# Windowed attention into a Fourier-mixing MLP: folding both DFTs by symmetry, reloading q and k as row runs

## The chip, the cores and the metric

The kernel runs on one core of a Trainium2 chip. Its engines are TensorE (PE, with its weight loads PEld), VectorE (DVE), ScalarE (ACT), GpSimd (POOL) and SyncE (SP); 16 DMA engines move data. The metric is device microseconds for one launch: 533.88 us, the median of three runs (532.82 to 534.48).

## The reference, cut to what matters

Inputs are q, k, v of shape (4 batches, 8 heads, 768 rows, 64), eight memory keys and values for each head, and the MLP's weights 512x2048 and 2048x512. Outputs are (4, 768, 512), all float32.

```
for c in range(24):                                  # chunks of 32 query rows
    k_full = concat(mem_k, k[32c-16 : 32c+40])       # clipped at the ends; v_full alike
    a = softmax(q[32c : 32c+32] @ k_full.T / 8)
    out[32c : 32c+32] = a @ v_full
x = heads side by side                               # (4, 768, 512)
mixed = real(fft(fft(x, axis=1), axis=2))
u  = x + mixed
un = (u - mean(u)) / sqrt(var(u) + 1e-6)             # over the 512 columns
y  = u + relu(un @ w_ch1) @ w_ch2
```

The real part of the two-dimensional DFT is C768 x C512 - S768 x S512, with C and S the cosine and sine tables. So it is two matrix products with 768-row tables, then two with 512-row tables.

## The kernel before, in words

Engines run their own instruction streams in order. The code is written per batch, and a scheduler fixes each stream's order at compile time: it interleaves the attention of batch b+1 with the Fourier part of batch b, as far as buffers allow. The calls at the end are attention(0), then for each b attention(b+1) and fx(b).

**Attention** (`emit_attention`, L148 to L215). Heads go in pairs. POOL issues DMAs that load q, k and v and cast on the way (L157 to L181); in DRAM one row of a head is 256 bytes. PE transposes q and k in 128-row tiles (L168, L172), ACT copies them to `qkTx`. Scores `p12` come in twelve blocks of 96 keys by 64 queries for each head (L194), and the memory keys are two more matmuls with 32 columns of weights (L187, L190). ACT takes two exponentials (L198, L200), PE multiplies by v with a column of ones (L205, tile `xa`, one PSUM buffer), and DVE divides by the sum (L212, L213), a reciprocal and a product for each 64-row half. The result lies in `xsb`, of which there are three, one for each batch in flight.

**Fourier part** (`emit_fx`, L217 to L284). x is split into fp16 high and low parts (`xh` L227, `xl` L228). For each of four 128-column tiles, 12 matmuls for the cosine (`pa`) and 12 for the sine (`pb`), each 392 columns wide (L236, L238), give the row DFT transposed for rows 0 to 391; the other rows follow by reflection. ACT and DVE split these into high and low again (L241 to L244), and DVE writes reflected copies `rrev` (L249). The column DFT (L267) is 16 matmuls of 512 columns for each of six row tiles `kt`, into `pm`. DVE then adds x (L270), takes mean and variance (L272, L273), ACT and DVE take 1/sqrt (L275, L276) and DVE subtracts the mean (L277). After all six tiles, PE transposes (L283) and DVE copies (L284) to `unT`.

**MLP** (L286 to L303). Two halves of 384 rows: 16 groups of four matmuls with relu on ACT (L290, L293), then three groups of 16 matmuls of 512 columns (L298). The factor 1/sqrt(var) is applied on DVE at the output (L301), where u is added too.

All matmul accumulators of fx share the tag `acc` in `fps`, with two PSUM buffers. The tables come from Sin on ACT at the start (L114, L118), beside the first attention; each switch between Sin and Exp loads a table. The two weight DMAs are the first on POOL's queue (L125, L126).

Of the kernel before, what the change touches and what calls it, by code (L numbers as in the profile page):

```python
# [10 lines left out]
FP32 = mybir.dt.float32  # L12
BF16 = mybir.dt.bfloat16
# [8 lines left out]
BIGM = 800.0  # L22


@with_exitstack
def kernel(
# [52 lines left out]
    tmem = cpool.tile([P, 2], FP32)
    nc.gpsimd.affine_select(out=tmem, in_=mbias, compare_op=ALU.is_ge, fill=0.0,  # L80
                            base=95, pattern=[[0, 2]], channel_multiplier=-1)
    nc.gpsimd.affine_select(out=mbias, in_=tmem, compare_op=ALU.is_ge, fill=-BIGM / 8.0,
                            base=103, pattern=[[0, 2]], channel_multiplier=-1)

    xsb = {}

    cs_sb = wpool.tile([P, NST, KM], FP16)
    ss_sb = wpool.tile([P, NST, KM], FP16)
    cd_sb = wpool.tile([P, NDT, DM], FP16)
    nsd_sb = wpool.tile([P, NDT, DM], FP16)  # L90
    sd_sb = wpool.tile([P, NDT, DM], FP16)
    krep = cpool.tile([P, S], FP32)
    nc.gpsimd.iota(krep, pattern=[[1, S]], base=0, channel_multiplier=0,
                   allow_small_or_imprecise_dtypes=True)
    with tc.tile_pool(name="trig", bufs=1) as tpool:
        def gen_trig(n_free, nt, NN, cout, sout, neg_sin):
            inv = 1.0 / float(NN)
            sc = 2.0 * math.pi / NN
            for t in range(nt):
                sv = tpool.tile([P, 1], FP32, tag="sv")  # L100
                nc.gpsimd.iota(sv, pattern=[[1, 1]], base=t * P, channel_multiplier=1,
                               allow_small_or_imprecise_dtypes=True)
                tsb = tpool.tile([P, 512], FP32, tag="tsb", bufs=1)
                ysb = tpool.tile([P, 512], FP32, tag="ysb", bufs=1)
                rsb = tpool.tile([P, 512], FP32, tag="rsb", bufs=1)
                tt = tsb[:, 0:n_free]
                yt = ysb[:, 0:n_free]
                rt = rsb[:, 0:n_free]
                nc.vector.tensor_scalar(tt, krep[:, 0:n_free], sv, None, ALU.mult)
                nc.vector.tensor_scalar(yt, tt, inv, None, ALU.mult)  # L110
                nc.vector.tensor_scalar(rt, yt, FSC, FSC, ALU.add, ALU.subtract)
                nc.vector.scalar_tensor_tensor(rt, rt, float(NN), tt, ALU.mult, ALU.subtract)
                ssc = sc if neg_sin else -sc
                nc.scalar.activation(sout[:, t, 0:n_free], rt, AFT.Sin, bias=0.0, scale=ssc)  # L114
                nc.vector.tensor_scalar(yt, tt, inv, 0.25, ALU.mult, ALU.add)
                nc.vector.tensor_scalar(rt, yt, FSC, FSC, ALU.add, ALU.subtract)
                nc.vector.scalar_tensor_tensor(rt, rt, float(NN), tt, ALU.mult, ALU.subtract)
                nc.scalar.activation(cout[:, t, 0:n_free], rt, AFT.Sin, bias=hpi_b, scale=-sc)  # L118
        gen_trig(KM, NST, S, cs_sb, ss_sb, neg_sin=False)
        gen_trig(DM, NDT, DM, cd_sb, nsd_sb, neg_sin=True)  # L120
    nc.vector.tensor_scalar(sd_sb, nsd_sb, -1.0, None, ALU.mult)
# [3 lines left out]
    nc.gpsimd.dma_start(w1_sb, moe_w_ch1.rearrange("(dt p) f -> p dt f", p=P))  # L125
    nc.gpsimd.dma_start(w2_sb, moe_w_ch2.rearrange("(ht p) m -> p ht m", p=P))  # L126

    qkTx = [apool.tile([P, KWQ + S], BF16, name=f"qkTx{i}") for i in range(NBUF)]
    va = [apool.tile([P, NT, 66], FP32, name=f"va_{i}") for i in range(2)]
    for i in range(NBUF):  # L130
        nc.vector.memset(qkTx[i][:, 0:LEFT], 0.0)
        nc.vector.memset(qkTx[i][:, LEFT + S:KW + NMEM], 0.0)
        nc.vector.memset(qkTx[i][:, KW + NMEM:KWQ], 0.0)
    for i in range(2):
        nc.vector.memset(va[i][:, :, 0:66], 0.0)
        nc.vector.memset(va[i][0:96, :, 64:65], 1.0)
        nc.vector.memset(va[i][0:16, 0, 64:65], 0.0)
        nc.vector.memset(va[i][64:96, NT - 1, 64:65], 0.0)
        nc.vector.memset(va[i][64:80, NT - 1, 64:65], 1.0)
        nc.vector.memset(va[i][96:104, :, 64:65], 1.0)  # L140
# [76 lines left out]
    def emit_fx(b):  # L217
# [122 lines left out]
```

## Time and profile before

The page is of one profiled execution with a span of 530.8 us from the first instruction to the last. The page gives no separate total for it; the timed median is 533.88 us, so 3.1 us lie around the span.

| what | value |
|---|---|
| span of the profiled execution | 530.8 us |
| timed median (three runs) | 533.88 us |
| PE busy | 440.5 us, 83% |
| DVE, ACT, POOL busy | 207.6, 190.9, 146.8 us |
| chain that ended last, PE's share | 71% |
| of that L290, L298, L267 | 17%, 16%, 15% |

Busy times of PE count a matmul from its start to its modelled end, and matmuls overlap; the pace of a run of matmuls is read from the time of the run over its count. The chain's rows give this pace directly.

### The profile page before, as it was taken

To read this page: it belongs to the slowest core of one execution; us is meant where nothing else is said; L and a number is where in the kernel's file an instruction comes from. 1 tells how busy PE (TensorE), PEld (TensorE's weight loads), DVE (VectorE), ACT (ScalarE), POOL (GpSimd) and SP (SyncE) were. 2 spreads that over 40 slices of the span, in tenths; PEclk is the share of its full clock that TensorE was granted. 3 is DMA by queue.
4 is the path that set the end of the run, shared out by engine and by line. 5 is a ranking of instruction groups with operands and counts; after the bars stand their busy time and mean duration, and the time that the engine had idled before them with its cause. 6 is when DMAs were issued, how large, how long until landed. Compare 5 with 4: busy or idle time off the path is not lost.

```text
span 530.8 us, 7916 instructions
## 1 busy us (share of the span) xinstructions
PE 440.5 (83%) x3184; PEld 242.5 (46%) x3184; DVE 207.6 (39%) x451; ACT 190.9 (36%) x343; POOL 146.8 (28%) x218
## 2 busy tenths in 40 slices
PE   0044358688998999999989999989979997997996
PEld 0023236455554545556446455654444544444453
DVE  7246552533656022252861115347631042452101
ACT  2169884223343615243215251542032501004250
POOL 5356643576555100266522011520000000000000
PEclk9999999999999899999997999999979999999999
DMA  7968551395546211366513111710000110000101
GB/s 140 195 74 84 63 55 49 57 97 71 71 68 42 23 44 33 91 95 79 54 13 26 41 37 65 97 49 0 1 0 22 40 61 0 1 0 1 40 21 59
DMA packets 66243, 27.28 MB, mean 51 GB/s; under 512 B 57504, under 2 KB 60576, under 8 KB 66208
## 3 DMA queue, kind: packets, MB, share of 16 engines
q0 software_dynamic: 58400, 19.58, 29.7%
q1 hardware_dynamic: 7808, 7.21, 4.1%
q8 instruction: 25, 0.41, 0.3%
q14 instruction: 10, 0.08, 0.1%
HBM read 31.00 MB, written 6.29 MB: 70 GB/s over the span
## 4 chain that ended last, share of the span: by engine, by line
PE 71%; ACT 10%; DMA 5%; POOL 5%; issue 4%; DVE 4%; ACTq 0%; POOLq 0%
PE ph L290 17%; PE pc L298 16%; PE pm L267 15%; PE pa L236 5%; PE pb L238 4%; DMA w_sb<-in_moe_w_ch_dram 4%; PE xa L205 4%; PE p L194 4%; PE tp L283 2%; PE trp L172 2%; PE trp L168 1%; ACT L118 1%; ACT L198 1%; ACT L200 1%; PE p L187 1%
## 5 line engine op out<-in xcount | busy, mean ns | idle before, releaser
L290 PE MATMUL ph<-unT,w_sb 128*128 128x384 f16 x512 | 97.8, 332 | 1.5 <-ACT hT L293 0.7
L293 ACT ACTIVATE hT<-ph 128x384 f16<-128x384 f32 x128 | 62.4, 491 | 86.5 <-PE ph L290 86.5
L298 PE MATMUL pc<-w_sb,hT 128*128 128x512 f16 x384 | 84.2, 379 | 0.0
L290 PEld LDWEIGHTS <-w_sb 128*128 128x128 f16 x512 | 49.4, 98 | 42.0 <-issue 14.0
L301 DVE SCALAR_TENSOR_TENSOR osb<-pc,rstd_s,xsb 128x512 f32<-128x512 f32 x24 | 18.0, 750 | 117.4 <-PE pc L298 117.1
L298 PEld LDWEIGHTS <-hT 128*128 128x128 f16 x384 | 37.5, 98 | 44.9 <-issue 0.6
L205 PE MATMUL xa<-va,e 128*64 128x66 f32 x768 | 37.3, 255 | 23.7 <-ACT e L200 23.1
L205 PEld LDWEIGHTS xa<-va,e 128*64 128x64 f32 x768 | 31.7, 163 | 35.0 <-ACT e L200 24.3
L175 POOL DMA_DIRECT2D va<-in_v_dram x32 | 17.8, 555 | 107.1 <-PE xa L205 103.5
L176 POOL DMA_DIRECT2D va<-in_v_dram x32 | 25.8, 806 | 55.0 <-PE trp L163 40.8
L236 PE MATMUL pa<-cs_sb,xh 128*128 128x392 f16 x96 | 32.4, 337 | 10.4 <-DVE r1l L243 6.8
L212 DVE RECIPROCAL zsum<-xa 64x6 f32<-64x6 f32 x64 | 12.3, 192 | 61.5 <-PE xa L205 60.7
L213 DVE TENSOR_TENSOR xsb<-xa,zsum 64x384 f32<-64x384 f32 x64 | 35.5, 554 | 1.9
L236 PE MATMUL pa<-cs_sb,xl 128*128 128x392 f16 x96 | 32.2, 336 | 0.9 <-DVE xl L228 0.9
L238 PE MATMUL pb<-ss_sb,xl 128*128 128x392 f16 x96 | 32.3, 337 | 0.0
L238 PE MATMUL pb<-ss_sb,xh 128*128 128x392 f16 x96 | 32.3, 336 | 0.0
L194 PEld LDWEIGHTS <-qkTx 64*96 64x96 bf16 x384 | 24.6, 146 | 15.1 <-issue 10.2
L157 POOL DMA_DIRECT2D q2b<-in_q_dram x32 | 29.8, 931 | 6.1 <-PE trp L168 5.8
L275 ACT ACTIVATE rsq<-mu_s,eps_b 128x1 f32<-128x1 f32 x24 | 7.1, 295 | 66.8 <-DVE mu_s L273 66.8
L241 ACT CAST r<-pa 128x392 f16<-128x392 f32 x16 | 7.8, 486 | 63.4 <-PE pa L236 63.4
L159 POOL DMA_DIRECT2D k2b<-in_k_dram x32 | 29.0, 907 | 1.2 <-PE trp L172 1.1
L194 PE MATMUL p<-qkTx 64*96 64x64 bf16 x384 | 28.4, 229 | 0.7
(93 smaller groups left out, 612.7 us busy)
## 6 DMA issues: line engine op xcount, KB each, us to landing
out_dram<-osb SPq DMA_DIRECT2D x24, 256.0 KB, 2.0
va<-in_v_dram POOLq DMA_DIRECT2D x32, 176.0 KB, 3.4
w_sb<-in_moe_w_ch_dram POOLq DMA_DIRECT2D x2, 2048.0 KB, 17.4
q2b<-in_q_dram POOLq DMA_DIRECT2D x32, 96.0 KB, 3.2
k2b<-in_k_dram POOLq DMA_DIRECT2D x32, 96.0 KB, 3.3
va<-in_v_dram POOLq DMA_DIRECT2D x32, 88.0 KB, 2.9
va<-in_mem_v_dram SPq DMA_DIRECT2D x32, 24.0 KB
va<-in_v_dram SPq DMA_DIRECT2D x32, 4.0 KB, 1.8
```

The lines of the kernel that those rows point to most:

```text
L157: nc.gpsimd.dma_start(q2b[:, :, hj, :], q[b, h + hj].rearrange("(t p) d -> p t d", p=P))
L159: nc.gpsimd.dma_start(k2b[:, :, hj, :], k[b, h + hj].rearrange("(t p) d -> p t d", p=P))
L176: nc.gpsimd.dma_start(v1[0:64, 1:NT, 0:D], v[b, h, 48:48 + (NT - 1) * 64].rearrange("(t p) d -> p t d", p=64))
L194: nc.tensor.matmul(p12[0:96, t, :], kqx[r0:r1_, t * 64:t * 64 + 96], kqx[r0:r1_, KWQ + t * 64: KWQ + t * 64 + 64], start=True, stop=True, ...
L205: nc.tensor.matmul(xa[rr:rr + 64, t // 2, 0:66], e1[:, t, :], v1[:, t, :], start=True, stop=True)
L213: nc.vector.tensor_tensor(xsb[b][rr:rr + 64, :, hc:hc + D], xa[rr:rr + 64, :, 0:D], zs.unsqueeze(2).to_broadcast([64, NST, D]), ALU.mult)
L236: nc.tensor.matmul(pa[:, 0:KM], lx, cs_sb[:, st, :], start=(im == 0), stop=(im == nmm - 1))
L238: nc.tensor.matmul(pb[:, 0:KM], lx, ss_sb[:, st, :], start=(im == 0), stop=(im == nmm - 1))
L267: nc.tensor.matmul(pm, lhs, rhs[:, dt, :], start=(im2 == 0), stop=(im2 == nmm2 - 1))
L290: nc.tensor.matmul(ph[:, 0:384], w1_sb[:, dt, ts(ht, P)], unT[:, dt, sh * 384:(sh + 1) * 384], start=(dt == 0), stop=(dt == NDT - 1))
L293: nc.scalar.activation(hT[:, ht, :], ph[:, 0:384], AFT.Relu)
L298: nc.tensor.matmul(pc, hT[:, ht, ts(stl, P)], w2_sb[:, ht, :], start=(ht == 0), stop=(ht == NHT - 1))
```

## The change

It rewrites the tile function. What the new code does:

- **Loads.** q and k of a head pair come uncast, as fp32, in runs of eight rows (2 KB) to 96 partitions (`qf`, `kf`, two buffers); POOL casts them to bf16 (L231, L233). All q, k, v and memory loads are issued by SP (L108 to L119). The 32 rows of v that the next block shares are copied on POOL (L237) and not loaded twice. `va` has four buffers.
- **Weights.** Eight DMAs on POOL's queue after the third head pair (`emit_weights`).
- **Attention.** Eight transposes each for q and k; memory keys are transposed once for all heads (`emit_mem_keys`) and stand inside each 128-column key block, so the scores are twelve matmuls per head with 128 columns of weights (L259) and nothing else. One reciprocal and one product per head (L274, L276). `xsb` has two buffers.
- **Row and column DFT.** x is folded on DVE before the products. `zy` adds or subtracts the two column halves (even and odd output columns), `pq` adds or subtracts the two row halves (even and odd output rows), `ff` adds or subtracts the reflected columns. For each of two column parities the row DFT is 24 matmuls of 193 columns (L312), plus 12 with one column of weights at parity 0 (L319). The column DFT is 8 matmuls of 256 columns per row tile (L341).
- **Norm.** Each row tile is transposed as soon as its mean is taken off (L353). 1/sqrt(var) is taken on POOL once per batch (L356, L357).
- **Order.** The calls are now pairs of batch 0, fx(0), then for each b: pairs of b+1, fx(b+1), mlp(b). `acc` has three buffers and serves the transposes too. The tables are half as wide and use one row of Sin calls.

The core of the diff:

```diff
+        nc.sync.dma_start(qf[n % NS], q[b, h:h + 2].rearrange("h (p j) d -> p h (j d)", j=RB))
+        nc.sync.dma_start(kf[n % NS][2:2 + QP], k[b, h:h + 2].rearrange("h (p j) d -> p h (j d)", j=RB))
+        for hh in range(2):
+            v1 = va[(2 * n + hh) % NV]
...
+            nc.sync.dma_start(v1[64:72, 0:NT, 0:D],
+                              mem_v[b, h + hh].unsqueeze(1).to_broadcast([NMEM, NT, D]))
...
+            xs[b] = apool.tile([P, NST, DM], FP32, tag="xsb", bufs=2, name=f"xsb{b}")
...
+        nc.gpsimd.tensor_copy(qb.rearrange("p j h d -> p h j d"),
+                              qf[n % NS].rearrange("p h (j d) -> p h j d", j=RB))
...
+            nc.gpsimd.tensor_copy(v1[96:128, 0:NT, 0:D], v1[0:32, 1:NB, 0:D])
...
-                nc.tensor.matmul(p12[96:128, 0:8, :], kqx[r0:r1_, KW:KW + 32],
-                                 kqx[r0:r1_, KWQ:KWQ + 512], start=True, stop=True,
-                                 tile_position=(r0, 96))
...
+                nc.tensor.matmul(sc[hh][:, t, :], kT[r0:r0 + 64, t * BS:t * BS + P],
+                                 qT[r0:r0 + 64, ts(t, 64)], start=True, stop=True,
+                                 tile_position=(r0, 0))
...
+            zy = fpool.tile([P, NST, HD], FP32, tag="fold", bufs=3, name="zy")
+            nc.vector.tensor_tensor(zy, xb[:, :, 0:HD], xb[:, :, HD:DM], op)
+            pq = fpool.tile([P, NST, HD], FP32, tag="fold", bufs=3, name="pq")
+            nc.vector.tensor_tensor(pq[:, 0:3], zy[:, 0:3], zy[:, 3:6], ALU.add)
+            nc.vector.tensor_tensor(pq[:, 3:6], zy[:, 0:3], zy[:, 3:6], ALU.subtract)
...
+            prev = rev_ap(pq, HD - 1, P - 1, [[HD, NST]])
+            nc.vector.tensor_tensor(ff[:, 0, :, 1:P], pq[:, :, 1:P], prev, opA)
+            nc.vector.tensor_tensor(ff[:, 1, :, 1:P], pq[:, :, 1:P], prev, opB)
...
+            nc.scalar.copy(hi.rearrange(fl), ff.rearrange(fl))
+            nc.vector.tensor_tensor(lo.rearrange(fl), ff.rearrange(fl), hi.rearrange(fl),
+                                    ALU.subtract)
...
+                            nc.tensor.matmul(ps[:, sp, :], part[:, ab, sp * 3 + st, :],
+                                             tab[:, sp, st, :], start=(st == 0 and i == 0),
+                                             stop=(st == 2 and i == 1))
...
+                nc.scalar.copy(rhv, ps)
+                nc.vector.tensor_tensor(up[:, 1].rearrange("p k s -> p s k"), ps, rhv,
+                                        ALU.subtract)
+                nc.vector.tensor_copy(dn, rev_ap(up, HS, HS, [[2 * NK, 2]]))
...
+                        nc.tensor.matmul(pm[:, par, :], lhs, rhs[:, par, :],
+                                         start=(im == 0), stop=(im == 3))
...
+            tp = fps.tile([P, NDT, P], FP16, tag="acc", name="tp")
+            for dt in range(NDT):
+                nc.tensor.transpose(tp[:, dt, :], un[:, ts(dt, P)], ident_h)
+            nc.vector.tensor_copy(unT[:, :, ts(kt, P)], tp)
...
-    emit_attention(0)
+    for i in range(HP):
+        emit_pair(i)
+        if i == HP - 2:
+            emit_weights()
+    emit_fx(0)
     for b in range(B):
         if b + 1 < B:
-            emit_attention(b + 1)
-        emit_fx(b)
+            for i in range(HP):
+                emit_pair((b + 1) * HP + i)
+            emit_fx(b + 1)
+        emit_mlp(b)
```

Three places in the engines' streams matter below. The first is DVE in the loop over row tiles `kt` of the last batch. `xsb` is that batch's x and u, `st` and `mu_s` its statistics. Before, from the fifth tile's add on:

```order
L270 TENSOR_TENSOR xsb_2851<-pm,xsb_2851 128x512
L272 BN_STATS st_4148<-xsb_2851 128x6
L273 BN_AGGR mu_s<-st_4148 128x2
L277 TENSOR_SCALAR un<-xsb_2851,mu_s 128x512
L276 RECIPROCAL rstd_s<-rsq 128x1
L270 TENSOR_TENSOR xsb_2851<-pm,xsb_2851 128x512
L272 BN_STATS st_4172<-xsb_2851 128x6
```

and now, the same tile:

```order
L345 TENSOR_TENSOR xsb_2759<-pm,xsb_2759 128x2x256
L347 BN_STATS st_3362<-xsb_2759 128x6
L348 BN_AGGR mu_s<-st_3362 128x2
L350 TENSOR_SCALAR un<-xsb_2759,mu_s 128x512
L354 COPY unT<-tp 128x4x128
L345 TENSOR_TENSOR xsb_2759<-pm,xsb_2759 128x2x256
L347 BN_STATS st_3383<-xsb_2759 128x6
```

The copy of the transposed tile now stands inside the loop, and the reciprocal has left DVE. The second place is PE in the same loop. Before, the end of one row tile and the start of the next; all 96 matmuls of the batch follow one another like this:

```order
L267 LDWEIGHTS rrev_3924
L267 MATMUL pm<-sd_sb,rrev_3924 128x512
L267 LDWEIGHTS rrev_3925
L267 MATMUL pm<-sd_sb,rrev_3925 128x512
L267 LDWEIGHTS rrev_3922
L267 MATMUL pm<-cd_sb,rrev_3922 128x512
```

and now, the end of the third row tile's products, its transposes and the start of the next tile's:

```order
L341 LDWEIGHTS up
L341 MATMUL pm<-nsinD,up 128x256
L353 LDWEIGHTS un
L353 MATMUL tp<-ident_h,un 128x128
...
L353 MATMUL tp<-ident_h,un 128x128
L341 LDWEIGHTS dn
L341 MATMUL pm<-cosD,dn 128x256
```

The next tile's products now stand behind the transposes of the tile before. The third place is DVE around the first batch's MLP, whose outputs are the `osb` rows. Before (`xsb_1784` is batch 2):

```order
L301 SCALAR_TENSOR_TENSOR osb<-pc,rstd_s,xsb_280 128x512 x3
L212 RECIPROCAL zsum<-xa 64x6
L155 MEMSET mk_2114 16x64
L213 TENSOR_TENSOR xsb_1784<-xa,zsum 64x6x64
L212 RECIPROCAL zsum<-xa 64x6
L213 TENSOR_TENSOR xsb_1784<-xa,zsum 64x6x64
L228 TENSOR_TENSOR xl<-xsb_717,xh 128x3072
L301 SCALAR_TENSOR_TENSOR osb<-pc,rstd_s,xsb_280 128x512 x3
```

and now (`xsb_1807` is batch 2):

```order
L354 COPY unT<-tp 128x4x128
L379 SCALAR_TENSOR_TENSOR osb<-pc,rstd,xsb_209 128x512 x6
L249 COPY kTb_84<-mkT 128x12x8
L276 TENSOR_TENSOR xsb_1807<-xa,zs 128x6x64
L274 RECIPROCAL zs<-xa 128x6
L276 TENSOR_TENSOR xsb_1807<-xa,zs 128x6x64
L274 RECIPROCAL zs<-xa 128x6
L276 TENSOR_TENSOR xsb_1807<-xa,zs 128x6x64
```

Before, attention products of batch 2 stood ahead of and between the MLP's outputs; now all six outputs stand first, and batch 2's first product comes behind them.

## Rows read from the trace of the kernel before

**Rows 1.** Page, busy time of each engine: us, share, instructions.

```profile
PE 440.5 (83%) x3184; PEld 242.5 (46%) x3184; DVE 207.6 (39%) x451; ACT 190.9 (36%) x343; POOL 146.8 (28%) x218
```

**Rows 2.** Chain of waits in time order: start us, length us, what.

```profile
4.35 21.61 DMA w_sb<-in_moe_w_ch_dram
...
33.17 1.18 PE p L194 x12
34.42 1.28 ACT L198
...
83.78 1.59 PE xa L205 x24
...
137.41 2.75 issue
...
218.98 0.85 PE xa L205 x24
...
435.53 0.99 PE pa L236 x6
...
455.98 20.89 PE pm L267 x96
...
484.38 9.80 PE ph L290 x56
...
516.43 10.37 PE pc L298 x48
```

**Rows 3.** Groups by form: line, operation, shapes, count | busy us, mean ns | idle before.

```profile
L270 DVE TENSOR_TENSOR xsb<-pm,xsb 128x512 f32<-128x512 f32 x24 | 16.6, 691 | 26.5 <-PE pm L267 26.4
L228 DVE TENSOR_TENSOR xl<-xsb,xh 128x3072 f16<-128x3072 f32 x4 | 13.4, 3358 | 30.0 <-PE ph L290 29.9
L272 DVE BATCH_NORM_STATS2 st<-xsb 128x6 f32<-128x512 f32 x24 | 16.7, 694 | 0.7
L273 DVE BATCH_NORM_AGGREGATE mu_s<-st 128x2 f32<-128x6 f32 x24 | 4.4, 182 | 0.8
L277 DVE TENSOR_SCALAR un<-xsb,mu_s 128x512 f16<-128x512 f32 x24 | 12.5, 520 | 0.8
L249 DVE COPY rrev<-r 128x1536 f16<-128x1536 f16 x8 | 4.7, 582 | 0.0
L213 DVE TENSOR_TENSOR xsb<-xa,zsum 64x384 f32<-64x384 f32 x64 | 35.5, 554 | 1.9
L198 ACT ACTIVATE e<-p,mbias 128x384 f32<-128x384 f32 x32 | 18.6, 581 | 15.3 <-PE p L194 12.7 <-PE xa L205 2.3
L170 ACT COPY qkTx<-trp 128x768 bf16<-128x768 bf16 x16 | 12.8, 799 | 37.4 <-PE trp L168 37.4
L241 ACT CAST r<-pa 128x392 f16<-128x392 f32 x16 | 7.8, 486 | 63.4 <-PE pa L236 63.4
L93 POOL IOTA krep<- 128x768 f32 x1 | 0.8, 771 | 0.0
L65 POOL CAST ident_h<-ident 128x128 f16<-128x128 f32 x1 | 0.3, 310 | 0.0
```

**Rows 4.** Timeline: start us, length us, engine, line, operation, count [idle before].

```profile
4.63 1.09 DVE L111 TENSOR_SCALAR rsb<-ysb 128x392 f32<-128x392 f32 x1
31.98 0.36 DVE L111 TENSOR_SCALAR rsb<-ysb 128x392 f32<-128x392 f32 x1 [0.38 <-ACT cs_sb L118]
101.60 1.76 DVE L227 CAST xh<-xsb 128x3072 f16<-128x3072 f32 x1
388.54 0.80 PE L283 MATMUL tp<-ident_h,un 128*128 128x128 f16 x6 [1.17 <-DVE unT L284]
479.99 0.49 PE L283 MATMUL tp<-ident_h,un 128*128 128x128 f16 x6 [0.65 <-DVE unT L284]
```

**Rows 5.** PE alone by stretch: from:to us, length, busy (count), granted clock, DMA.

```profile
387.00:388.00 1.00, 0.37 (x2) 0.50 0.00 0
479.00:481.00 2.00, 1.05 (x9) 1.00 0.00 0
```

**Rows 6.** Page, the queue that SP's loads use: packets, MB, share of 16 engines.

```profile
q1 hardware_dynamic: 7808, 7.21, 4.1%
```

More of the change, by code (lines that the diff above doesn't have):

```diff
@@ L22, with rev_ap, strided @@
 BIGM = 800.0
+def rev_ap(src, last, count, outer=()):
+    dims = [list(src.ap[0])] + [list(d) for d in outer] + [[-1, count]]
+    return bass.AP(tensor=src.tensor, offset=src.offset + last, ap=dims)
+def strided(src, off, dims):
+    return bass.AP(tensor=src.tensor, offset=src.offset + off,
+                   ap=[list(src.ap[0])] + [list(d) for d in dims])
 @with_exitstack
@@ new lines, with pairs_of @@
+    NV = 4
+    va = [spool.tile([P, NB, 66], FP32, name=f"va{i}") for i in range(NV)]
+    NKT = 2
+    kTb = [spool.tile([P, NB * BS], BF16, name=f"kTb{i}") for i in range(NKT)]
+    pair_order = {0: [0, 2, 1, 3]}
+    def pairs_of(b):
+        return pair_order.get(b, list(range(H // 2)))
+    seq = [(b, pr) for b in range(B) for pr in pairs_of(b)]
+    for i in range(NS):
+        nc.gpsimd.memset(kf[i], 0.0)
+    for i in range(NKT):
+        nc.gpsimd.memset(kTb[i], 0.0)
+    for i in range(NV):
+        nc.vector.memset(va[i], 0.0)
+        nc.vector.memset(va[i][0:64, :, 64:65], 1.0)
+        nc.vector.memset(va[i][0:16, 0, 64:65], 0.0)
+        nc.vector.memset(va[i][64:72, :, 64:65], 1.0)
+        nc.vector.memset(va[i][96:128, :, 64:65], 1.0)
+        nc.vector.memset(va[i][96:128, NT - 1, 64:65], 0.0)
+        nc.vector.memset(va[i][96:112, NT - 1, 64:65], 1.0)
@@ L82 @@
[L82 to L93, printed above, removed]
-                   allow_small_or_imprecise_dtypes=True)
@@ L95 @@
[L95 to L120, printed above, removed]
@@ new lines, with reduced @@
+    sv = cpool.tile([P, 3], FP32)
+    nc.gpsimd.iota(sv, pattern=[[P, 3]], base=0, channel_multiplier=1,
+                   allow_small_or_imprecise_dtypes=True)
+    def reduced(tt, n, NN, name):
+        y = fpool.tile([P, n], FP32, name=f"y{name}", tag="fold", bufs=3)
+        nc.vector.tensor_scalar(y, tt, 1.0 / float(NN), FSC, ALU.mult, ALU.add)
+        nc.vector.tensor_scalar(y, y, FSC, float(NN), ALU.subtract, ALU.mult)
+        nc.vector.tensor_tensor(tt, y, tt, ALU.subtract)
+        ab = fpool.tile([P, n], FP32, name=f"a{name}", tag="fold", bufs=3)
+        nc.vector.scalar_tensor_tensor(ab, tt, -1.0, tt, ALU.mult, ALU.max)
+        return tt, ab
@@ new lines @@
+    ttS = fpool.tile([P, 3, 2, NK], FP32, tag="fold", bufs=3, name="ttS")
+    for st in range(3):
+        nc.vector.tensor_scalar(ttS[:, st], kk[:, :, 0:NK], sv[:, st:st + 1], None, ALU.mult)
+    nS = 3 * 2 * NK
+    r, ab = reduced(ttS.rearrange("p a b c -> p (a b c)"), nS, S, "S")
+    scS = 2.0 * math.pi / S
+    for par in range(2):
+        rp = r.rearrange("p (a b c) -> p b a c", a=3, b=2)[:, par]
+        abp = ab.rearrange("p (a b c) -> p b a c", a=3, b=2)[:, par]
+        nc.scalar.activation(sinS[:, par], rp, AFT.Sin, bias=0.0, scale=-scS)
+        nc.scalar.activation(cosS[:, par], abp, AFT.Sin, bias=hpi_b, scale=-scS)
@@ L129 @@
[L129 to L140, printed above, removed]
```

341 lines of the change are left out of this document (181 added, 160 removed).

## The prediction

> **What bounds the kernel now.** I read the page's busy times first, then the chain of waits in time order, the groups by form for durations, the timeline for single operations, and the granted clock in two stretches. PE is busy 83% of the span and DVE 39% [rows 1], so PE looks like the bound. The chain says where that holds. From 145 us on it is nearly all PE: 96 matmuls of the column DFT take 20.89 us (218 ns each, PE without a gap), six of the row DFT 0.99 us (165 ns each), 48 of the MLP's second product 10.37 us (216 ns each) [rows 2]. Before that it is not PE. It starts with 21.61 us of weight DMA, which stands ahead of the first v; then ACT loads a table of 1.28 us at each switch between Exp and Sin (one stands at 34.42); around 137 us the chain waits on POOL's issue of DMAs, 2.75 us at a time [rows 2]. The first operation of fx(0) on DVE starts at 101.60 [rows 4].
>
> The last batch shows a cycle without attention beside it: fx from 435.53 to 484.38, 48.9 us, then an MLP that ends in matmuls at 516.43 + 10.37 = 526.8, 42.4 us [rows 2].
>
> PE has two paces. Six transposes take 0.80 us at 388.54 and 0.49 us at 479.99 [rows 4]; the granted clock at 387 to 388 is 0.50 (1.2 GHz), after a stretch in which PE had mostly waited for the last row tile's mean, and 1.00 (2.4 GHz) at 479 to 481 [rows 5]. The 24 matmuls of `xa` took 1.59 us at 83.78 and 0.85 us at 218.98 [rows 2], so the first attention ran at the slow pace.
>
> **The change part by part.**
>
> *PE's columns.* Row DFT per batch: 96 matmuls of 392 columns (15.8 us at 165 ns) become 60 of 193 (by proportion 81 ns, 4.9 us). Column DFT: 96 of 512 (20.9 us) become 48 of 256 (109 ns, 5.2 us). That takes 26.6 us per batch off PE, 106 us in all. The two memory-key matmuls per head go too. If PE stayed the bound, the time would be near 533.88 - 106 = 428, before anything at the start. It doesn't stay the bound, for the rest of this part.
>
> *DVE's fold.* A product of two tensors costs 691 ns for 512 elements and 3358 ns for 3072 [rows 3], that is 157 + 1.042 per element. For each parity `zy` (1536) is 1757 ns, `pq` 2 x 957, `ff` 2 x 951 and a copy of 80, `lo` (1536) 1757, two `up` rests (386) 2 x 559. The reflected copy `rrev` of 1536 took 582 [rows 3]; I take 360 for each of two of 768. Sum 9.25 us, 18.5 for both parities, and all of it lies ahead of the first column product but what waits on PE or ACT. ACT adds `hi` (from 486 ns for 392 and 799 for 768 [rows 3], 0.83 per element, 1.44 us for 1536) and casts of 0.49.
>
> The chain from the last attention product to the first add of u: fold of parity 0 and first `lo` end at 9 us, since the fold of parity 1 fills the wait for `hi`. In PE's order only one matmul of each of the two row products may run before `lo`, so 34 remain: 34 x 81 ns = 2.8 us at full pace, 5.5 at half. Then the cast on ACT; the second `hi` stands behind both casts of parity 0 on ACT, so at half pace it starts at 15.2 and the second `lo` ends at 18.4; 24 matmuls (2 or 4 us), cast, rest, reflected copy, four matmuls. First add at 24 us with half pace, 20 with full.
>
> *The loop over row tiles.* Before, 16 matmuls of one tile (3.48 us) covered DVE's work on the tile before: 691 + 694 + 182 + 520 = 2.09 us [rows 3]. Now the next tile's products stand behind this tile's transposes, and those wait for the mean, so the two add. Per tile at full pace: 8 x 109 ns + 0.17 until the last result + 2.09 + five handovers of some 0.05 + four transposes (0.49 / 6 each, and pipelined, 0.2) = 3.5 us, just what the 16 matmuls took. At half pace 8 x 218 + 0.2 + 2.34 + 0.43 = 4.6 us. PE works about a third of such a cycle at full pace; in [rows 5] it worked 0.37 us of a microsecond at the half clock and stayed at full clock in the other stretch, so the trace has both ends. I take half pace, since the loop has a wait of over 2 us in each of six tiles. The Trainium skill ("TensorE: Matmul & The Clock Gate", Part 1) says that the half clock is the default and that work releases it; the drop in rows 5 agrees. By it all six tiles would run slow, which is the value I take; if the rule did not hold here, rival A's sum would.
>
> So fx alone: 24 + 2.3 to the first transposes + 5 x 4.6 = 49.3, less one for bursts that reach full pace: 48 us (41 at full). With pieces of attention in PE's and DVE's order, in fx(0) and fx(1): 50.
>
> *Attention.* `xsb` has two buffers now. Batch b+2's products write the buffer that MLP(b) reads at its output, so from batch 2 on they wait for the MLP's end, and `xa` (one buffer) waits with them. Before, three buffers let it run beside the MLP. So each fx has attention ahead of it, exposed: one head is `xa` 0.85 + reciprocal and product 0.75 + handovers, 1.8 us [rows 2, 3], and a pair that must still be transposed and scored needs at half pace 16 transposes (2.1), an ACT copy (0.8), 24 score matmuls (12 took 1.18 [rows 2]; 2.4), two Exp at 0.581, `xa` 1.59, product 0.75, `xa` 1.59: 10.4 us, 7 at full. Ahead of fx(1): two heads and one pair, 14. Ahead of fx(2): seven heads and scores for three pairs, between 13 (seven heads alone) and 26; 19. Ahead of fx(3): seven heads, one pair beside them, 13. On DVE half of the 64 reciprocals and products go, 6 us per batch, hidden beside PE before.
>
> *The start.* The weights no longer stand ahead of v, and Sin comes in one piece. First Exp at about 23 us (between 13, where loads and casts alone would end, and 34.42, where it stands); first pair done at 28; three more at 10 each, in series by PE's order: fx(0) starts at 58, instead of 101.6. The lower end is 48 (all at full pace), the upper 75.
>
> *Loads and POOL.* Rows of v are 256 bytes still. The hardware queue took 0.041 x 16 x 530.8 / 7808 = 45 ns per packet and engine [rows 6]; a pair now has 2112, 5.9 us on 16 engines, less than its 7 to 10 us. POOL's casts (1024) and copies (768) have no row of their size: the iota of 768 took 771 ns, the cast of 128 took 310 [rows 3]. By the first a pair costs 3.6 us, by the second in proportion 8.7. I take 4.6, nearer to the row of like size. Either hides, but in the start. Eight weight DMAs stand ahead of the last pair's casts, some 7 us, just covered.
>
> *MLP.* Unchanged, 42; after a slow fx its first matmuls run at half pace, 44 for the first three; the last follows another MLP.
>
> **Sum.** 58 + 50 + 14 + 50 + 44 + 19 + 48 + 44 + 13 + 48 + 44 + 42 + 1 (last output) = 475 us of span, against 530.8. With the 3.1 around it: 478 us.
>
> **The rivals.**
>
> *A. Full pace throughout.* PE keeps 2.4 GHz in the loop over tiles, as at 479 to 481. Then 55 + 43 + 12 + 43 + 42 + 17 + 41 + 42 + 12 + 41 + 42 + 42 + 1 = 433, 436 in all. Against it stands the half clock at 387 after one such wait, where the new loop has six.
>
> *B. The fold does nothing for the end and the loads spoil the start.* fx is 48 to 50 either way, and 2112 short packets per pair take three times the mean because weights (8 MB) run beside them: 18 us per pair, fx(0) at 58 + 32 and some later pairs late by 10: 520. For it, 256-byte rows; against it, 45 ns was the mean of a queue that already carried such rows.
>
> *C. Slower: POOL and DVE block each other.* POOL's casts and copies now run while DVE folds. At 4.63 a DVE operation took 1.09 us beside a DMA issue on POOL, 0.36 alone [rows 4]. If every microsecond of POOL (16 x 4.6 = 74) took one of DVE on the chain, the time would be 478 + 74 = 552. It decides above 56 us, three quarters of it. Against it: the product L213 kept a mean of 554 ns over 64 [rows 3] with POOL issuing all along. The Trainium skill ("GPSIMD Engine Reference", Specifications) says that POOL shares its SBUF interfaces with VectorE and contends with instructions of two SBUF inputs; the fold's are such. The slow L111 agrees in kind; no row here shows it for a cast.
>
> *D. No change.* The start's 44 us are gone in any case, so this needs +55 elsewhere: 0.02.
>
> **How the numbers follow.** Main case 0.52 (own range 455 to 500), A 0.28 (425 to 455), B 0.12 (500 to 530), C 0.06, D 0.02. Range 432 to 510: it leaves out a part of A below, C, D and half of B. About 0.3% is what this measurement can tell from no change. Faster 0.92, same 0.02, slower 0.06.
>
> **What would show it.** Right: fx(0)'s first `zy` near 58; `zy` about 1.76 us; about 4.6 us from one `pm` add to the next with the granted clock at 0.50; batch 2's products after the MLP's outputs; PE busy far below 83%. Wrong: adds 3.5 us apart (A); v or q waits of SP's DMAs on the chain in the first 90 us (B); `zy` or `lo` far above 1.76 (C). If attention hides beneath the MLP after all, 46 us of my sum fall away.

## The result and the profile after

The kernel after takes 495.95 us, the median of five runs (494.58 to 500.56), beside 532.82 for the kernel before (five runs, 532.28 to 534.48): a ratio of 0.931, 95% interval 0.928 to 0.935. That is 37 us less where 55 were forecast. The profiled execution is the longest of the five: 500.56 us, span 498.6, so 2.0 us lie around the span. The median one has a span of 494.0; what is read below from the trace is thus of an execution 4.6 us longer, and no trace shows where those lie.

The page: busy time of each engine, the granted clock in 40 slices, and the shares of the chain.

```profile
PE 340.6 (68%) x2848; PEld 221.8 (44%) x2848; DVE 207.1 (42%) x365; ACT 150.6 (30%) x258; POOL 90.8 (18%) x99
...
PEclk9999999676556569999756558999757559999999
...
PE 57%; DVE 22%; DMA 7%; issue 6%; ACT 4%; SPq 2%; POOL 2%; POOLq 0%; ACTq 0%; DVEq 0%
```

PE lost 100 us of work against [rows 1], the span 32. PE now idles for 158 us (498.6 - 340.6), 90 before. A slice is 12.5 us, so the clock's valleys lie at 87 to 187 (fx(0) and fx(1)), 237 to 312 (fx(2)) and 349 to 411 (the attention ahead of fx(3), and fx(3)). Stretch by stretch (from:to, length, busy time of PE, PEld, DVE, ACT and POOL, granted clock, DMA share, GB/s): fx(1), the MLP behind it, fx(2), and the row tiles of fx(2) alone.

```profile
132.60:186.00 53.40, 30.94 (x269) 23.04 (x269) 35.42 (x55) 14.07 (x20) 5.81 (x6) 0.55 0.22 53
186.00:228.00 42.00, 41.43 (x225) 21.67 (x223) 4.66 (x7) 15.72 (x32) 5.68 (x6) 1.00 0.24 69
251.20:301.50 50.30, 28.74 (x197) 20.63 (x197) 34.50 (x52) 8.25 (x11) 6.00 (x6) 0.53 0.10 25
280.00:299.00 19.00, 9.62 (x50) 5.85 (x48) 10.26 (x21) 0.00 (x0) 0.00 (x0) 0.50 0.00 0
```

In the MLP PE is full at 2.4 GHz. In fx(1) and fx(2) no engine is full and PE runs at 1.2 GHz for nearly all of it; fx(3) is like them (granted clock 0.57), fx(0) is not (0.81). The timeline (start, length, engine, line, operation, idle time before it and its releaser) gives the table load ahead of the first Exp, the first fold, batch 2's first product, one row tile of fx(2) from add to add, and in fx(3) the first `zy` and the first add:

```profile
25.67 1.28 ACT L266 ACT_TABLE_LOAD   x1 [0.95 <-PE sc L259]
63.42 2.58 DVE L290 TENSOR_TENSOR zy<-xsb 128x1536 f32<-128x1536 f32 x1
...
228.12 0.56 DVE L276 TENSOR_TENSOR xsb<-xa,zs 128x384 f32<-128x384 f32 x1
...
284.97 0.69 DVE L345 TENSOR_TENSOR xsb<-pm,xsb 128x512 f32<-128x512 f32 x1 [1.28 <-PE pm L341]
287.18 0.60 PE L353 MATMUL tp<-ident_h,un 128*128 128x128 f16 x4 [2.25 <-DVE un L350]
288.86 0.63 PE L341 MATMUL pm<-sinD,dn 128*128 128x256 f16 x2
289.53 0.69 DVE L345 TENSOR_TENSOR xsb<-pm,xsb 128x512 f32<-128x512 f32 x1 [1.28 <-PE pm L341]
...
360.82 1.76 DVE L290 TENSOR_TENSOR zy<-xsb 128x1536 f32<-128x1536 f32 x1
...
384.23 0.69 DVE L345 TENSOR_TENSOR xsb<-pm,xsb 128x512 f32<-128x512 f32 x1
```

The two rows at 284.97 and 289.53 answer to the adds L270 of before [rows 3]: 4.57 us apart, PE waits 2.25 for DVE and DVE 1.28 for PE, in turn. fx(0) starts at 63.42; before, its first operation stood at 101.60 [rows 4]. That is 38.2 us, more than the whole gain of 32.2 between the two profiled executions: from there to the end it is 429.2 us before and 435.2 after. Behind the start the change, the folded DFTs with the new order and buffers, gave nothing back. fx(3), with no attention beside it, takes 49.1 us; the last fx of before took 48.9 [rows 2].

The chain of waits (start, length, what) in the start and between MLP(0) and fx(2):

```profile
28.11 1.58 PE xa L271 x24
...
50.66 14.93 DMA kf<-in_k_dram
65.65 7.60 DMA kf<-in_k_dram
73.31 7.74 DMA kf<-in_k_dram
...
227.33 0.75 DVE osb L379
...
228.73 0.94 PE xa L271 x24
...
251.22 1.77 DVE zy L290
```

Of the 30 us of `kf`, the first 15 fall while the weights load (their DMAs are issued from 36.6 on and the last lands at 66.8); the other two waits come behind. Batch 2's first product (228.12) stands right behind the last output of MLP(0) (`osb`, 227.33).

Which part of the new start gives the 38 us is not shown by a run of its own. In the trace of before ACT loads a table 20 times in the first 80 us, 25.6 us in all, and in after three times, 3.8 us; the 21.6 us of weights ahead of the first v [rows 2] are gone too. What the row runs of q and k give was not tested.

### The profile page after: what moved, and what is told of

It reads as the page before. It is cut to its first block, busy times and chain, and to the rows that moved or that the text cites. A ratio compares the mean times of both kernels' runs of the same rounds, so it can differ in the third digit from the quotient of the medians.

```text
span 498.6 us, 6910 instructions
## 1 busy us (share of the span) xinstructions
PE 340.6 (68%) x2848; PEld 221.8 (44%) x2848; DVE 207.1 (42%) x365; ACT 150.6 (30%) x258; POOL 90.8 (18%) x99
## 4 chain that ended last, share of the span: by engine, by line
PE 57%; DVE 22%; DMA 7%; issue 6%; ACT 4%; SPq 2%; POOL 2%; POOLq 0%; ACTq 0%; DVEq 0%
PE ph L368 17%; PE pc L376 17%; PE pm L341 7%; DMA kf<-in_k_dram 6%; PE xa L271 5%; PE ps L312 5%; DVE xsb L345 3%; DVE st L347 3%; PE tp L353 3%; DVE zy L290 2%; DVE lo L304 2%; DVE un L350 2%; DVE xsb L276 1%; PE sc L259 1%; SPq L116 1%
## 5 line engine op out<-in xcount | busy, mean ns | idle before, releaser
L379 DVE SCALAR_TENSOR_TENSOR osb<-pc,rstd,xsb 128x512 f32<-128x512 f32 x24 | 18.0, 751 | 151.6 <-PE pc L376 151.6
L271 PE MATMUL xa<-va,e 128*64 128x65 f32 x768 | 43.9, 285 | 30.4 <-issue 13.2
L237 POOL COPY va<-va 32x768 f32<-32x768 f32 x32 | 32.5, 1029 | 100.8 <-DMA va<-in_v_dram 100.1
L266 ACT ACTIVATE e<-sc,mbias 128x384 f32<-128x384 f32 x64 | 32.4, 581 | 48.1 <-PE xa L271 31.1
L353 PE MATMUL tp<-ident_h,un 128*128 128x128 f16 x96 | 13.7, 293 | 39.9 <-DVE un L350 39.8
L312 PE MATMUL ps<-cosS,hi 128*128 128x193 f16 x48 | 15.8, 358 | 25.3 <-ACT hi L303 25.3
L356 POOL TENSOR_SCALAR rstd<-mu_s 128x6 f32<-128x6 f32 x4 | 2.0, 491 | 166.8 <-DVE mu_s L348 166.8
L244 ACT COPY qT<-trp 128x768 bf16<-128x768 bf16 x16 | 12.8, 800 | 62.5 <-PE trp L242 62.5
L259 PE MATMUL sc<-qT,kTb 64*128 64x64 bf16 x384 | 14.1, 224 | 25.0 <-ACT kTb L252 23.8
L353 PEld LDWEIGHTS <-un 128*128 128x128 f16 x96 | 7.8, 125 | 47.4 <-DVE un L350 47.0
L274 DVE RECIPROCAL zs<-xa 128x6 f32<-128x6 f32 x32 | 6.2, 194 | 51.6 <-PE xa L271 51.6
L231 POOL CAST qb<-qf 96x1024 bf16<-96x1024 f32 x16 | 18.7, 1166 | 46.8 <-PE trp L242 41.7
L345 DVE TENSOR_TENSOR xsb<-pm,xsb 128x512 f32<-128x512 f32 x24 | 16.6, 692 | 24.5 <-PE pm L341 24.3
L312 PEld LDWEIGHTS <-hi 128*128 128x128 f16 x96 | 12.7, 139 | 27.7 <-ACT hi L303 26.8
L259 PEld LDWEIGHTS <-kTb 64*128 64x128 bf16 x384 | 11.0, 116 | 30.1 <-ACT kTb L252 26.6
```

Of the source, the lines that this page charges most:

```text
L231: nc.gpsimd.tensor_copy(qb.rearrange("p j h d -> p h j d"), qf[n % NS].rearrange("p h (j d) -> p h j d", j=RB))
L237: nc.gpsimd.tensor_copy(v1[96:128, 0:NT, 0:D], v1[0:32, 1:NB, 0:D])
L259: nc.tensor.matmul(sc[hh][:, t, :], kT[r0:r0 + 64, t * BS:t * BS + P], qT[r0:r0 + 64, ts(t, 64)], start=True, stop=True, tile_position=(r0 ...
L266: nc.scalar.activation(e1[:, :, ts(c, 32)], sc[hh][:, :, ts(c, 32)], AFT.Exp, bias=mbias[:, c:c + 1], scale=1.0 / math.sqrt(D))
L271: nc.tensor.matmul(xa[rr:rr + 64, t // 2, 0:65], e1[:, t, :], v1[:, t, 0:65], start=True, stop=True)
L312: nc.tensor.matmul(ps[:, sp, :], part[:, ab, sp * 3 + st, :], tab[:, sp, st, :], start=(st == 0 and i == 0), stop=(st == 2 and i == 1))
```

## The experiments

Times are medians of four runs (of three in e4, whose fourth took 497.77 us); ratios are to the kernel before in runs beside them (medians 533.7 to 534.1), with 95% intervals. For "after" the number to compare is 495.95 (0.931). Expectations name two accounts, a theory and a rival. Stages are read from one trace each.

**e1, the kernel before with a cleaner start.**

```diff
+    nc.vector.scalar_tensor_tensor(mbias, cd_sb[:, NDT - 1, 0:2], 0.0, mbias, ALU.mult, ALU.add)
...
-    nc.gpsimd.dma_start(w1_sb, ...)      # and w2_sb
...
     emit_attention(0)
+    nc.gpsimd.dma_start(w1_sb, ...)      # and w2_sb
```

> The kernel before with two edits at its start only: the weight DMAs are issued after the first batch's attention, and a product that writes the Exp bias reads the last Sin table, so that no Exp can stand between Sins (no table switches). Theory (the whole measured gain is the start, the folded DFT returns nothing after it): fx(0) starts at 62 to 72 us instead of 101.6 and the rest keeps its 429 us, so 494 to 506 us. Rival (the start is hidden behind other work and the folded DFT brings the gain): not below 520 us.

521.01 us, ratio 0.977 (0.974 to 0.980). By the number it is the rival's side (not below 520), but the start that the theory asked for did not come either. The last table load and the first operation of fx(0), in the timeline:

```profile
47.23 1.28 ACT L197 ACT_TABLE_LOAD   x1 [0.28 <-DVE mbias L122]
...
90.85 1.76 DVE L226 CAST xh<-xsb 128x3072 f16<-128x3072 f32 x1
```

It stands 10.75 us earlier than before, not 30 to 40: the old table code is a long series on DVE, and with the edit the first Exp waits for its end at 47 (in before the first stands at 35.7). But the span is 12.3 us shorter, so what the start gives reached the end in full here, against the rival's reason that it is hidden. That the start explains all of the change's 37 us is thus shown by the two traces, and by e1 only as a rate (10.75 us give 12.3) at a third of the size.

**e2, three `xsb` buffers**; room comes from `mkf` and `mkb`, which move into tiles that are free at the start.

```diff
-  tag="xsb", bufs=2
+  tag="xsb", bufs=3
```

> The kernel after with three xsb buffers instead of two (the memory keys' staging tiles take the place of buffers that are free at the start). Theory (attention of batch 2 and 3 is exposed ahead of fx because its products wait for the MLP that reads the same buffer): the stretches of 23.9 and 16.7 us between an MLP and the next zy shrink to under 8 each, fx takes 3 to 5 us more because it holds those matmuls, 460 to 472 us. Rival (PE runs at half clock in fx, so what moves into it lengthens it by as much): 488 to 498 us.

472.86 us, ratio 0.885 (0.882 to 0.888): 23.1 us less than after, 0.9 outside the theory's range. The timeline between MLP(0) and fx(2):

```profile
220.74 0.75 DVE L379 SCALAR_TENSOR_TENSOR osb<-pc,rstd,xsb 128x512 f32<-128x512 f32 x1 [2.70 <-PE pc L376]
...
230.27 2.39 DVE L290 TENSOR_TENSOR zy<-xsb 128x1536 f32<-128x1536 f32 x1
```

From MLP(0)'s last output to the next `zy` it is now 9.5 us (under 8 was expected); in after, from 227.33, 23.9. Ahead of fx(3) it is 7.2 instead of 16.7. fx(2), which holds more of the attention, takes 53 us instead of 50.3; fx(1), which now holds products of batch 2, takes 48 instead of 53.2, with its adds 3.5 to 3.9 us apart at a granted clock of 1.00. The theory's mechanism holds: attention was exposed by the buffer, and fx takes it for nothing in sum. The full clock in the loop of fx(1) has its part in that.

**e3, transposes one row tile late.**

```diff
-            tp = ... ; 4 transposes of un ; copy to unT
+            uns.append(un)
+            if kt >= 1:
+                emit_tp(kt - 1)          # the same five instructions, for the tile before
```

> The kernel after with the four transposes and the copy of row tile kt written one tile later, behind the eight pm matmuls of kt+1. Theory (pm and DVE's chain of a tile add up because the next pm stands behind this tile's transposes in PE's order): from add to add 4.57 falls to 2.6 to 3.1 us, 6 to 8 us per fx, 464 to 474 us. Rival (the loop is bound by the half clock or by DVE's five operations with their handovers): add to add stays above 4 us, 488 to 498 us.

463.36 us, ratio 0.867 (0.864 to 0.870): 32.6 us less than after, 0.6 below the theory's range. The adds of fx(2) in the timeline (the first row holds two):

```profile
263.43 1.29 DVE L353 TENSOR_TENSOR xsb<-pm,xsb 128x512 f32<-128x512 f32 x2 [0.45 <-PE pm L349]
...
268.93 0.69 DVE L353 TENSOR_TENSOR xsb<-pm,xsb 128x512 f32<-128x512 f32 x1 [1.28 <-PE pm L349]
270.53 0.69 DVE L353 TENSOR_TENSOR xsb<-pm,xsb 128x512 f32<-128x512 f32 x1
273.70 0.69 DVE L353 TENSOR_TENSOR xsb<-pm,xsb 128x512 f32<-128x512 f32 x1 [0.42 <-PE pm L349]
275.24 0.67 DVE L353 TENSOR_TENSOR xsb<-pm,xsb 128x512 f32<-128x512 f32 x1
```

Five steps in 11.8 us, 2.4 us each (2.6 to 3.1 were expected), and they come in pairs. The two waits no longer add. The granted clock of 262 to 278 was 0.86, so part of this is the clock, 1.05 us of a step by e4.

**e4, weights after fx(0).** `emit_weights()` moves from behind the third pair to behind `emit_fx(0)`.

> The kernel after with the eight weight DMAs issued after fx(0) instead of after the third head pair. Theory of the prediction (loads hide, the start is a chain of pairs in series by engine order): first zy at 58 to 62 instead of 63.4, total 488 to 496 us. Rival B's mechanism (8 MB of weights beside the short packets of v, q and k hold back kf, which stands 30 us in the chain between 50 and 81): first zy at 50 to 56, the kf waits gone, zy(1) at 112 to 120 instead of 132.6, total 475 to 485 us.

492.71 us, ratio 0.921 (0.918 to 0.923): 3.2 us less, inside the theory's range. First `zy` at 62.77, as the prediction's theory has it. Of the `kf` waits one of 4.57 us is left ahead of fx(0), and fx(0)'s last add comes at 108.16 instead of 115.53. But then POOL's eight issues, 4.6 us of the chain between 112 and 117, delay the casts of the attention ahead of fx(1), whose `zy` comes at 131.37. Rival B's mechanism exists: of the 7.4 us that the last add gains, 4.8 lie between `zy` and the first add, 1.9 in steps of the loop at a higher clock and 0.7 in the start. The place that avoids it costs most of that again.

This trace also gives the clock's price by itself. In fx(2) PE does nothing in a step from add to add but four transposes and eight `pm`, in after's order. The first step (the two adds, then as a stretch) ran at full clock, the last three at half (columns as above):

```profile
268.68 0.69 DVE L345 TENSOR_TENSOR xsb<-pm,xsb 128x512 f32<-128x512 f32 x1
...
272.20 0.69 DVE L345 TENSOR_TENSOR xsb<-pm,xsb 128x512 f32<-128x512 f32 x1 [0.45 <-PE pm L341]
...
268.68:272.20 3.52, 1.27 (x12) 0.93 (x12) 2.48 (x7) 0.00 (x0) 0.00 (x0) 1.00 0.00 0
276.77:290.47 13.70, 6.94 (x36) 4.39 (x36) 7.44 (x15) 0.00 (x0) 0.00 (x0) 0.50 0.00 0
```

That is 3.52 us at 1.00 and 4.57 (13.70 / 3) at 0.50 for the same matmuls: 1.05 us a step.

**e5, PE kept busy in the loop over row tiles.**

```diff
+            for _ in range(28):
+                nc.tensor.transpose(tp[:, 0, :], ident_h, ident_h)
             for dt in range(NDT):
                 nc.tensor.transpose(tp[:, dt, :], un[:, ts(dt, P)], ident_h)
```

> The kernel after with 28 extra transposes of the identity ahead of the four real ones of each row tile, into the same PSUM tile, which the real ones overwrite: work that needs nothing and only keeps PE busy while the tile's mean is computed. Rival A's price (at full clock a tile takes 3.5 to 3.7 us): the granted clock in the loop goes to 1.00, add to add from 4.57 to 3.5 to 3.8 us, fx 5 to 6 us shorter, 472 to 482 us. Rival (the clock stays at half, the extra 28 take 3.0 us and stand in the way): add to add 5.0 to 5.5 us, 500 to 512 us.

479.78 us, ratio 0.900 (0.896 to 0.904): 16.2 us less, with 672 useless transposes more. The row tiles of fx(2) by stretch (columns as above):

```profile
275.00:294.00 19.00, 17.68 (x241) 15.04 (x240) 15.28 (x32) 0.68 (x2) 1.84 (x2) 1.00 0.01 2
```

And two adds with the fill between them in the timeline:

```profile
281.09 0.69 DVE L345 TENSOR_TENSOR xsb<-pm,xsb 128x512 f32<-128x512 f32 x1
282.67 0.38 PE L341 MATMUL pm<-sinD,dn 128*128 128x256 f16 x2
283.30 0.40 PE L355 MATMUL tp<-ident_h,un 128*128 128x128 f16 x4 [0.25 <-DVE un L350]
283.75 0.38 PE L341 MATMUL pm<-sinD,dn 128*128 128x256 f16 x2
283.97 1.73 PE L353 MATMUL tp<-ident_h 128*128 128x128 f16 x28
284.17 0.69 DVE L345 TENSOR_TENSOR xsb<-pm,xsb 128x512 f32<-128x512 f32 x1
```

The granted clock is 1.00 where it was 0.50, and add to add is 3.08 us, less than the expected 3.5. The edit is not pure: with the fill, the scheduler put four of the eight `pm` matmuls ahead of the transposes (282.67) and four behind (283.75), so a piece of the serial order went too. The clock's own price is read from e4 and e8, which keep the order.

**e6, e2 and e3 together.**

> Both edits, three xsb buffers and the transposes one tile late. If the two losses are apart (attention ahead of fx, and the serial loop in fx): 23.1 and 32.6 us add up, 436 to 444 us. Rival (the third buffer gained because attention filled the very waits in the loop that the later transposes remove): 448 to 460 us.

447.71 us, ratio 0.840 (0.836 to 0.844). The two edits give 48.2 of their 55.7 us, between the two expectations: most of each loss is its own. The other 7.5 us overlap; the same idle time, or the same gain of clock, counted twice would do it, and no run shows which.

**e7 and e8, groups of MLP(b) inside fx(b+1)**, with e2 and e3 (e7) or alone (e8). `emit_mlp` becomes a generator that yields after each group, and `emit_fx` draws from it:

```diff
+            pull(10 if par == 0 else 4)     # ahead of the row products
+                pull(3)                     # behind each row product
+            pull(2)                         # behind each row tile's pm
...
-            emit_fx(b + 1)
-        emit_mlp(b)
+            emit_fx(b + 1, m)               # m = emit_mlp(b)
+        for _ in m: pass
```

> Three xsb buffers, transposes one tile late, and the groups of MLP(b) written between the steps of fx(b+1) (10 groups ahead of the first row products, then 3, 4 and 3, two for each row tile, the rest behind). Theory (after the change no engine is full; fx is a chain of waits, and the MLP's 42 us of PE work could lie in it): fx with the MLP inside takes 58 to 75 us at full clock, 63 + 48 + 3 x 66 + 42 + 14 of attention = 365, so 360 to 395 us. Rival (the MLP's groups stand ahead of the fx chain's own matmuls and lengthen it by as much as they take): 425 to 440 us.

> The kernel after with the groups of MLP(b) written between the steps of fx(b+1) and nothing else (two xsb buffers, transposes in their place). Theory: three of the four MLPs lie beside an fx of 55 to 60 us, attention of 24 and 17 us stays exposed: 63 + 54 + 15 + 57 + 24 + 57 + 17 + 57 + 42 + 4 = 390, so 385 to 410 us. Rival (the groups stand ahead of the chain): 480 to 495 us.

e7: 396.71 us, ratio 0.744 (0.741 to 0.748). e8: 410.55, ratio 0.770 (0.768 to 0.773). e8 ends half a microsecond above its range and e7 1.7 above; both rivals are out by 28 and 70 us. In e7, the stretch from `zy` of fx(1) to `zy` of fx(2):

```profile
129.00:212.80 83.80, 73.16 (x740) 47.15 (x739) 43.32 (x79) 36.67 (x67) 15.94 (x17) 0.89 0.31 79
```

It holds a whole MLP, an fx and a batch of attention in 85 us (128.17 to 212.82); in after the same took 118.6 (132.61 to 251.22). PE is busy 87% of it. The time that the fold had freed on PE was there, but the code's order, MLP(b) behind fx(b+1), left it idle. (The 440.5 us of PE's work before [rows 1] would not have fitted into e7's 396.71.) The timeline of e8, fx(2), has all eight `pm` behind the transposes as in after, and MLP groups in PE's gaps:

```profile
261.18 0.69 DVE L353 TENSOR_TENSOR xsb<-pm,xsb 128x512 f32<-128x512 f32 x1 [0.45 <-PE pm L348]
263.40 0.40 PE L361 MATMUL tp<-ident_h,un 128*128 128x128 f16 x4 [0.53 <-DVE un L358]
263.63 0.38 PE L348 MATMUL pm<-cosD,up 128*128 128x256 f16 x2
264.50 1.30 PE L376 MATMUL ph<-unT,w_sb 128*128 128x384 f16 x7
264.71 0.69 DVE L353 TENSOR_TENSOR xsb<-pm,xsb 128x512 f32<-128x512 f32 x1 [0.45 <-PE pm L348]
```

From add to add it is 3.53 us, at a granted clock of 1.00 over 257 to 272, the step of e4 at full clock. So of a tile's 4.57 us the half clock is 1.04, and the eight `ph` matmuls in such a step cost the chain nothing. Elsewhere the MLP does cost: the last step, with `pc` matmuls in it, takes 5.20 us, and from `zy` to the first add it is 35.9 us instead of 24.6.

**e9, weights after the first pair**, where the trace of after shows a lull of the DMAs.

```diff
-        if i == HP - 2:
+        if i == 0:
             emit_weights()
```

> The kernel after with the eight weight DMAs issued after the first head pair, before POOL's casts of the second, so that they run between about 13 and 30 us, where the trace of after moves almost nothing. Theory (the weights cost the start only because they run beside the short packets of v, q and k): zy(0) stays at 60 to 64 (pairs in series), the 30 us of kf waits go, zy(1) at 118 to 125 instead of 132.6, 482 to 488 us. Rival (POOL's 7 us of issues delay the second pair and everything behind it): zy(0) at 66 to 72, 495 to 503 us.

493.38 us, ratio 0.922 (0.918 to 0.926): 2.6 us less, outside both ranges. `zy` at 59.74, but that of fx(1) at 128.6, not 118 to 125: the wait has moved from `kf` to v, as the chain of waits shows.

```profile
29.52 11.43 DMA va<-in_v_dram
41.03 6.33 DMA va<-in_v_dram
```

Either place of the weights leaves fx(0)'s start at 60 to 63; most of it is the pairs in series, as the prediction had it.

**e10, POOL made busy beside the fold**; `mkf` moves as in e2, for room.

```diff
+        for _ in range(8):
+            scr = fpool.tile([P, 2, DM], BF16, tag="scr", bufs=2, name="scr")
+            nc.gpsimd.tensor_copy(scr, xb[:, 0:2, :])
```

> The kernel after with eight extra POOL copies of 1024 elements per batch that read x as soon as attention has written it, into a scratch tile nobody reads: about 10 us of POOL beside each fold. Rival C's price (each microsecond of POOL takes one of DVE): 10 us per fx, 530 to 540 us. Theory (a DVE product of two tensors beside POOL takes 2.58 instead of 1.75 us, so ten microseconds of POOL cost some 3 us of DVE): fx(2) and fx(3) 2 to 4 us longer, fx(0) and fx(1) some more because POOL's casts stand behind, 503 to 516 us.

518.74 us, ratio 0.971 (0.967 to 0.974): 22.8 us more, 2.7 above the theory, 11 below rival C. The timeline in fx(2), then in fx(3) the first `zy` and the first add:

```profile
253.15 1.76 DVE L293 TENSOR_TENSOR zy<-xsb 128x1536 f32<-128x1536 f32 x1
253.25 16.17 POOL L285 CAST scr<-xsb 128x1024 bf16<-128x1024 f32 x8 [9.54 <-DVE xsb L276]
261.72 2.59 DVE L293 TENSOR_TENSOR zy<-xsb 128x1536 f32<-128x1536 f32 x1
264.23 2.58 DVE L307 TENSOR_TENSOR lo<-ff,hi 128x1536 f16<-128x1536 f32 x1
...
372.11 1.76 DVE L293 TENSOR_TENSOR zy<-xsb 128x1536 f32<-128x1536 f32 x1
...
400.62 0.69 DVE L348 TENSOR_TENSOR xsb<-pm,xsb 128x512 f32<-128x512 f32 x1 [0.16 <-PE pm L344]
```

Eight casts took 16.17 us (some 10 were expected), and the second `zy` and the first `lo` 2.6 where they take 1.75 alone; the first `zy`, which started 0.1 us ahead of the first cast, still took 1.76. fx(3), whose fold has no other POOL work beside it, needs 28.5 us from `zy` to the first add instead of 23.4: 5.1 us for 16 us of POOL, a third of rival C's price. fx(2) loses 9.2 there; its casts for batch 3 now stand behind the copies, which would explain the rest but was not tested.

**e11, e7 with the weights after the first pair.**

> Three xsb buffers, transposes one tile late, MLP groups inside the next fx, and the weights after the first head pair. If the start's loss is apart from the others, what the weights in the lull give alone comes off the 396.7 us: 384 to 391 us. Rival (with the MLP in fx(1), PE has work there in any case and the start's delay is already hidden): 394 to 398 us.

393.46 us, ratio 0.735 (0.732 to 0.738), the best version here. It lies between the two expectations (391 and 394), so it does not decide between them; the 3.2 us it gains on e7 are about e9's 2.6.

## Why the prediction was right, and where its sizes were off

The direction, the place of the gain and the reasons that held it small were right; 478 stood against 496. Two of its signs of being wrong came in part: waits on SP's loads stand on the chain in the first 90 us (rival B; v at 32.86 for 2.86 us, then `kf`), and `zy` took 2.58 in fx(0) (rival C). Neither was large enough to decide the time (e4, e10). By its own sum, in the profiled execution:

| term | forecast | measured |
|---|---|---|
| start to `zy` of fx(0) | 58 | 63.4 |
| fx(0) | 50 | 54.7 |
| attention ahead of fx(1) | 14 | 14.5 |
| fx(1) | 50 | 53.2 |
| MLP(0) | 44 | 42.3 |
| attention ahead of fx(2) | 19 | 23.1 |
| fx(2) | 48 | 50.3 |
| MLP(1) | 44 | 43.4 |
| attention ahead of fx(3) | 13 | 15.9 |
| fx(3) | 48 | 49.1 |
| MLP(2), MLP(3) | 86 | 85.3 |
| to the end | 1 | 3.4 |
| span | 475 | 498.6 |

**PE's columns.** PE's busy time fell by 100 us (106 forecast, at full pace), and as forecast that bounds nothing: e7 shows the freed time can be used, after does not use it.

**The fold and the chain to the first add.** Forecast 24 us at half pace; 23.4 in fx(3), where nothing runs beside it. In fx(2), fx(1) and fx(0) it took 24.6, 27.2 and 30.5. This is the first mis-sized step: the fold was priced alone, and one microsecond was added for attention. POOL works beside it (`zy` 2.58 at 63.42, 1.76 at 360.82), and in fx(0) PE's second row product stands behind six `xa` that wait 3.2 us. In fx(0) that is at a granted clock of 0.89 up to the add, not the half that the price assumed, so the clock hid part of the miss. Rival C's mechanism is real; e10 gives its price as a third of POOL's time. Between `zy` and the first add of fx(0) POOL is busy 16.0 us in after and 3.9 in e4, whose loads come sooner; at that price the difference makes 4 of the 4.8 us that e4 gains there (an estimate). So late loads would cost in the main by moving POOL's casts into the fold. The Trainium skill ("GPSIMD Engine Reference", Specifications) names this contention for instructions with two SBUF inputs; the trace agrees for most such products beside POOL (2.6 instead of 1.75), not for all (1.76 at 253.15, e10). L111, which the prediction set beside this, has one input tensor, so that row shows a slow DVE operation beside POOL's DMA issue, but no such product.

**The loop over row tiles.** Forecast 4.6 us at half clock and 3.5 at full; measured 4.57 at 0.50 in after, 3.52 at 1.00 in e4 and 3.53 in e8. That is closer than the working: its terms add to 4.71 and 3.58, so the fit is in part luck, by some 0.1 us a tile. Rival A's price was right, and it failed at the clock: it was 0.50 in most of fx(1) to fx(3). The Trainium skill ("TensorE: Matmul & The Clock Gate", Part 1) has the half clock as the default that work releases; the trace agrees both ways, after's loop at 0.50 and e5's, the same but for the fill and the four `pm`, at 1.00.

**Attention.** That batch b+2 waits for MLP(b) was right (e2). Ahead of fx(2), 23.1 instead of 19: the second mis-sized step. The first four heads took 1.85 each, as forecast (1.8). The transposes, copies and scores of three pairs stood in series with the other three, 16 us from 235.2 to 251.2; the prediction had set them between 0 and 13 us on top of the heads and taken half.

**The start.** The third, and the largest: 63.4 for 58. The three later pairs took 10 us each as forecast ((63.4 - 33.2) / 3 = 10.1), but the first was done at 33.2 (its second `xa` ends at 32.45) instead of 28: the first Exp came at 27, not 23, since the copy of the keys, the scores and a table load of 1.28 us follow the last Sin. The weights cost it 3.7 us at most (e9), and 0.7 by e4. Loads were said to hide but in the start; they held fx(0) up too (e4: from `zy` to its first add it is 25.7 us without weights beside it, 30.5 with them).

**Around the span** 2.0 us, not 3.1: the 3.1 set the median of three executions against the span of one, and in the later runs of before it is 1.7 for each; the end after the last product 3.4, not 1.

The miss of 23.6 us in the span is thus four terms of 3 to 5 us (start, fx(0), fx(1), attention ahead of fx(2)), 17 us together, and smaller ones of 1 to 3 (attention ahead of fx(3), the end, fx(2), fx(3)); but for the MLPs all lie on one side. Each was priced along its own chain, with too little for what runs beside it.

## What to carry to other kernels

Work taken off the fullest engine pays only where something else is ready to run on it: after such a change look at the stages again, for it may have turned a full engine into a chain of waits. Then the order of the code counts more than the work: a buffer fewer, a transpose ahead of the next products, or a stage written behind another cost 23 to 85 us here, each undone by a few lines. Price a stage beside its neighbours, not alone.

## What was not expected of the hardware

- Useless work made the kernel faster: with 672 extra transposes on PE the granted clock of the loop was 1.00 instead of 0.50, and 16.2 us went, a part of it by the four `pm` that moved ahead.
- POOL and DVE slow each other: a 1024-element cast on POOL took 2.0 us beside the fold, where casts of 1024 took 1.03 to 1.05 in after between fx(0) and fx(1), and DVE's product of 1536 elements 2.6 instead of 1.75.
